# Retention and routed experts on one core: the routing counts kept as separate tiles, and scalings and weight splits moved between VectorE and GpSimd

## The chip, the cores and the metric

The kernel runs on one core of a Trainium2 chip. The metric is the device time of one execution in microseconds (us). TensorE, VectorE, ScalarE, GpSimd and SyncE are called PE, DVE, ACT, POOL and SP in the profile. SP issues nearly all loads, POOL issues the scatters by index.

## What is computed

Four sequences of 768 tokens with 8 heads of 64 features go through a retention layer: a state per head decays by a factor gamma at each token and takes up the product of key and value, and the output is the query times the state. The 3072 output rows of 512 features then go through a layer of 8 experts, each token to the one expert with the largest gate logit:

```python
for t in range(S):
    state = gamma * state + einsum('bhd,bhe->bhde', k[:, :, t], v[:, :, t])
    y[:, :, t] = scale * einsum('bhd,bhde->bhe', q[:, :, t], state)
...
logits = x @ w_gate
expert_idx = argmax(logits, axis=1)
...
for e in range(E):
    mask = expert_idx == e
    h = maximum(x[mask] @ w1[e], 0.0)
    out[mask] = gate_w[mask, None] * (h @ w2[e])
```

## The kernel before

**Two stages.** The first (roughly the first 103 us) does the retention, the gate logits and the sorting of the rows by expert into a DRAM tensor, `x_sorted`. The second (`moe_main`) takes one expert after the other and is a dense run of matmuls. Between them the first 320 rows of expert 0 are already multiplied as "early pieces" (`fill`, L801 and L820), so that TensorE has work while the last rows are routed.

**The first stage** works on 24 chunks of 128 tokens, six per sequence, in a hand-written order. The loop of L539 has twelve rounds, n = 0 to 11, with chunks a = 2n and b = 2n + 1 each. For a chunk g there are:

- `load(g)` (L222): one DMA of 1 MB with q, k and v, on SP's queue, which takes its instructions in order. Chunks 0 to 3, 15 to 18 and 21 to 23 use the four buffers `qkv_t`; the others use `qkv_w`, whose buffers are later those of the split weights.
- `scale(g)` (L237): `vs`, the values times a decay, one TENSOR_TENSOR with 128x512 outputs and both inputs in SBUF, on DVE or on POOL. There are three buffers for `vs`, so vs(g) waits until vs(g-3) was read for the last time.
- `scores(g)` (L250): matmuls into the PSUM tiles `sp` (L256), then the causal mask on DVE into `Sb` (L259, two instructions per chunk; one input is in PSUM).
- `update(g)` (L263): matmuls of the keys with vs(g) into the state `U` (L271), then a copy `ub` on ACT (L274). The next update writes the same `U`.
- `carry(n)` and `output(g)` (L290, L303): the output `Y`; `evict(g)` (L306): `Y` times a decay into `xT` on DVE (L311).
- `logits` (L351), `rows` (L322: transposes into the PSUM banks "s0" and "s1", which the scores use too) and `finish_logits` (L363, L367) of the round before.

**Routing** goes by six groups of chunks (`GROUPS`): the first 6 chunks are routed in round 3, the next 6 in round 6, then 4 in round 8, 2 in round 9, 4 in round 11 and the last 2 after the loop. In a group `choose` (L390 to L399, DVE) finds the expert of each token as a one-hot matrix `Eb`, `rank` (L406 to L410, PE) adds up in PSUM tile `pf` the row of each token inside its expert's region, `slots` and `weights` (DVE) take the row and the gate weight out, `label` (L438, L439, ACT) writes weight and token number into the row, and `advance` (L420) adds the group's counts to `run`: a TENSOR_REDUCE (L422) and a TENSOR_TENSOR (L423, `run` + `tot`). `run` starts as each expert's first row, divided by 128 (L601).

**Scatters.** `send_behind(tile, chunks)` (L328) lets POOL copy one column of `tile` (`gated`, L330), which makes it wait for that tile, and then issues one scatter of 128 rows per chunk (L746). `BEHIND`, `AMID` and `AFTER` (L46 to L48) say which chunks in which round. Round 9 is `soon`: after it all rows of the first 18 chunks are sent, and `fetch_early` (L454) reads the first 320 rows of expert 0 back, which `turn_early` (L458) transposes in round 11 into `xt0`.

**Weight splits.** `fetch(0, part)` (L123) loads a quarter of expert 0's weights into `raw`, which has two buffers; `split` (L133) makes `whi` on ACT (L138) and `wlo` on DVE or POOL (L139, both inputs in SBUF). In the first stage it does one of four pieces (128x512) at a time. `_PIECES` (L53) says how many pieces fall in which round; L620 does them at the end of it, on DVE in rounds 5, 7 and 10 and on POOL otherwise. The pieces go in the order part 0 to 3, piece 0 to 3. Parts 2 and 3 are fetched at chunks 6 and 8 (`fetches`, L534), which are reached at the ends of rounds 3 and 4; `LATER` (L52) has the loads of chunks 15 to 20 there too.

**Where the scalings stand before.** In rounds 3, 4, 6, 7 and 8 (`BEHIND`) POOL does vs(a+4) ahead of the round's scatters (L598), and DVE does vs(b+2) after the evictions (L604). In round 9 DVE does vs(b+2) there and POOL vs(a+4) after the scores. In the other rounds POOL does both after the scores (L617, L619).

Of the kernel before, what the change touches and what calls it, by code (L numbers as in the profile page):

```python
# [9 lines left out]
F32 = mybir.dt.float32  # L10
# [39 lines left out]
FIRST = AHEAD + 11  # L50
MID = (19, 20)
LATER = {6: (15, 16), 7: (17,), 8: (18,), 9: (19,), 10: (20,)}  # L52
_PIECES = {2: 3, 3: 2, 5: 4, 6: 1, 7: 2, 9: 2, 10: 2}  # L53
_ORDER = iter([(part, i) for part in range(4) for i in range(4)])
SPLITS = {n: tuple(next(_ORDER) for _ in range(c)) for n, c in _PIECES.items()}
BIG = 1 << 20
# [44 lines left out]
def retention_moe(ctx, tc, qkv, w1, w2, cst, gdec, out):  # L101
# [102 lines left out]
    with ExitStack() as actx:  # L204
# [168 lines left out]
        def gating(i):  # L373
            a, w = GROUPS[i]
            total = a + w in (FULL, NCH)
            last = a + w == NCH
            sm = lambda name, n=1, dt=F32: gsm.tile([P, w, n], dt, name=f"{name}{w}")
            bc = lambda t, n=E: t.broadcast_to([P, w, n])
            span = slice(a, a + w)
            Eb, key, gw = EA[:, span, :], KEY[:, span, :], GW[:, span, :]  # L380
            NB = w + total
            v = {}
            ex = exs[:, 0:w]

            def choose():

                lg, eq, pr = [state["spare"][:, n * w * E:(n + 1) * w * E].rearrange("p (i e) -> p i e", e=E)
                              for n in range(3)]
                mx, ed = v["mx"], v["ed"] = sm("mx"), sm("ed")
                nc.vector.tensor_reduce(out=mx, in_=lgs[i], axis=AX.X, op=ALU.max)  # L390
                nc.vector.tensor_reduce(out=lg, in_=lgs[i].unsqueeze(3), axis=AX.X, op=ALU.add)
                nc.vector.tensor_tensor(out=eq, in0=lg, in1=bc(mx), op=ALU.is_equal)
                nc.vector.tensor_tensor(
                    out=pr, in0=eq, op=ALU.mult,
                    in1=k_("desc").unsqueeze(1).broadcast_to([P, w, E]))
                nc.vector.tensor_reduce(out=ed, in_=pr, axis=AX.X, op=ALU.max)
                nc.vector.tensor_tensor(out=Eb, in0=pr, in1=bc(ed), op=ALU.is_equal)
                v["sh"] = sm("sh", E)
                nc.vector.tensor_tensor(out=v["sh"], in0=lg, in1=bc(mx), op=ALU.subtract)  # L399

            def soft():
                nc.scalar.activation(out=ex[:, :, 0:E], in_=v["sh"], func=AF.Exp)

            def rank():
                pf = v["pf"] = bank(2, "pf", (P, NB, E)) if i < 3 else ps_1.tile([P, NB, E], F32, name="pf", tag="U" if i == 4 else "misc")
                nc.tensor.matmul(out=pf[:, 0:w, :], lhsT=us, rhs=Eb, start=True, stop=False, skip_group_check=True)  # L406
                nc.tensor.matmul(out=pf, lhsT=ones, rhs=run.unsqueeze(1).broadcast_to([P, NB, E]),
                                 start=False, stop=False, skip_group_check=True)
                for n in range(NB - 1):
                    nc.tensor.matmul(out=pf[:, n + 1:, :], lhsT=ones,  # L410
                                     rhs=Eb[:, n:n + 1, :].broadcast_to([P, NB - 1 - n, E]),
                                     start=False, stop=(n == NB - 2), skip_group_check=True)

            def slots():
                rk = sm("rk", E)
                nc.vector.tensor_tensor(out=rk, in0=v["pf"][:, 0:w, :], in1=Eb, op=ALU.mult)
                with nc.allow_low_precision(reason="one nonzero term, an integer below 2**15"):
                    nc.vector.tensor_reduce(out=key, in_=rk, axis=AX.X, op=ALU.add)

            def advance():  # L420
                tot = gsm.tile([P, E], F32, name="tot")
                nc.vector.tensor_reduce(out=tot, in_=Eb.rearrange("p i e -> p e i"), axis=AX.X, op=ALU.add)  # L422
                nc.vector.tensor_tensor(out=run, in0=run, in1=tot, op=ALU.add)  # L423

            def counts():

                dst, classes = (cnt, slice(0, E)) if last else (full, slice(0, 1))
                nc.vector.tensor_tensor(out=dst, in0=v["pf"][:, w, classes], in1=k_("ebase")[:, classes],
                                        op=ALU.subtract)

            def weights():
                nc.vector.tensor_reduce(out=gw, in_=ex, axis=AX.X, op=ALU.add)
                nc.vector.reciprocal(out=gw, in_=gw)

            def label():
                b, c = divmod(a, CPB)
                x = xrows[b][:, c:c + w]
                nc.scalar.copy(out=x[:, :, :, P + 1], in_=gw.broadcast_to([P, w, 4]))  # L438
                nc.scalar.copy(out=x.bitcast(I32)[:, :, :, P],  # L439
                               in_=k_("tok4")[:, span].unsqueeze(2).broadcast_to([P, w, 4]))  # L440

            return dict(choose=choose, soft=soft, rank=rank, slots=slots, advance=advance, counts=counts,
                        weights=weights, label=label)

        early, first, start_at = [], {}, []

        def start_rows():

# [82 lines left out]
        scale(2)  # L531

        last = NCH // 2 - 1
        fetches = {6: 2, 8: 3}  # L534
        chosen = {(a + w) // 2: i for i, (a, w) in enumerate(GROUPS) if a + w < NCH}
        soon = FULL // 2
        stages = {}
# [1 line left out]
        for n in range(last + 1):  # L539
# [8 lines left out]
            if n > 0:  # L548
                if n == last:
                    turn_early()  # L550
                if n != soon:
                    logits(n - 1)
                if n == last:
                    for j, w, _ in first["pieces"]:
                        cut_high(nc, first["x"][0], first["xt"], j, w)
                if n in AMID:
                    send_behind(state["LT"][:, 0:1], AMID[n])
                rows(a - 2, "s0")
                rows(a - 1, "s1")
                finish_logits(n - 1)  # L560
            if s and n < last:
                s["choose"]()
            if n == soon:
# [30 lines left out]
            elif s:  # L594
                for name in ("weights", "label")[2 * (n == soon):] + ("advance",):
                    s[name]()
            if n in BEHIND:
                scale(a + 4)  # L598
                send_behind(xTs[n][:, 0, C:C + 1], BEHIND[n])
            if n == 1:  # L600
                nc.vector.tensor_scalar(out=run, in0=k_("ebase"), scalar1=1.0 / P, scalar2=None, op0=ALU.mult)  # L601
            if n < last:
                if n in BEHIND or n == soon:
                    scale(b + 2, nc.vector)  # L604
                if n > 0:
                    update(a + 2)
# [6 lines left out]
            if n == 0:  # L613
                nc.scalar.copy(out=wgs[:, :, 0:E], in_=k_("gates").rearrange("p (k e) -> p k e", k=NP))
            if n < last:
                if n not in BEHIND and n != soon:
                    scale(b + 2)  # L617
                if n < last - 1 and n not in BEHIND:
                    scale(a + 4)  # L619
            for i in SPLITS.get(n, ()):  # L620
                split(0, *i, nc.vector if n in (5, 7, 10) else nc.gpsimd, 1)
            for g in (a, b):
                if FIRST <= g < NCH - AHEAD - len(MID):
                    load(g + AHEAD + len(MID))
# [585 lines left out]
```

## Time and profile before

| what | us |
|---|---|
| median of 3 runs (lowest, highest) | 400.54 (398.85, 401.35) |
| the profiled execution, its own time | 400.35 |
| span of its profile, from the first to the last instruction | 398.5 |
| what lies around the span | 1.85 |
| busy: PE, DVE, POOL, ACT | 386.5, 248.7, 176.8, 141.7 |
| mean granted clock of PE, as a share of 2.4 GHz | 0.994 |

Times in the rows below are microseconds from the start of the span. A timeline row has start, duration, engine, line, operation, output tile "<-" input tiles, sizes and how often it is repeated without a break; in square brackets stands how long the engine was idle before it and what ended that. A repeated row's duration runs from the first start to the last end. Ends of matmuls are modelled, so the step from one PE row's start to the next is the safer measure.

### The profile page before, as it was taken

What the parts mean: (1) busy time and instruction counts of PE and PEld (TensorE: products, weight loads), DVE (VectorE), ACT (ScalarE), POOL (GpSimd) and SP (SyncE); (2) the same over time, 40 slices, a digit from 0 to 9 for tenths busy, and PEclk for the clock granted to TensorE, in tenths of its full rate; (3) what the DMA queues carried; (4) which work ended last, traced back from release to release, by engine and by line L of the source; (5) the groups of instructions that cost most, each with busy time, mean ns of one, the idle gap of its engine ahead of it and who ended that gap; (6) DMA issues with size and microseconds to landing.
All of it is one profiled execution on the core that took longest, in us unless ns stands there. A gap on an engine that the chain in (4) does not pass through costs nothing. (4 is left out here: it accounts for less than half of the span.)

```text
span 398.5 us, 8280 instructions
## 1 busy us (share of the span) xinstructions
PE 386.5 (97%) x3260; PEld 359.7 (90%) x3260; DVE 248.7 (62%) x479; ACT 141.7 (36%) x248; POOL 176.8 (44%) x168
## 2 busy tenths in 40 slices
PE   8999999879999999999999999999999999999995
PEld 4888878668899879999999999999999999999984
DVE  3467587986754578583877377467738656675411
ACT  2234344333511446532542345144324415523200
POOL 1647918581160417400483067118505822850743
PEclk9999999998999999999999999999999999999999
DMA  7999999963047939656443846365474737530111
GB/s 276 420 419 419 415 422 420 422 273 69 2 162 161 361 137 256 233 208 140 180 156 123 192 145 251 61 189 208 147 183 131 251 71 216 178 136 1 48 54 47
DMA packets 42332, 81.53 MB, mean 205 GB/s; under 512 B 4460, under 2 KB 18160, under 8 KB 39860
## 3 DMA queue, kind: packets, MB, share of 16 engines
q1 hardware_dynamic: 36768, 67.46, 50.3%
q0 software_dynamic: 5376, 13.49, 9.0%
q8 instruction: 26, 0.43, 0.4%
q14 instruction: 14, 0.11, 0.1%
q10 hardware_dynamic: 148, 0.04, 0.0%
HBM read 65.90 MB, written 15.68 MB: 205 GB/s over the span
## 5 line engine op out<-in xcount | busy, mean ns | idle before, releaser
L746 POOL DMA_INDIRECT out<-Z,sidx x90 | 102.8, 1143 | 138.8 <-DVE Z L927 113.5
L139 DVE TENSOR_TENSOR wlo<-raw,whi 128x1024 fp32r<-128x1024 f32 (+1 forms) x62 | 70.5, 1146 | 14.2 <-ACT whi L138 13.9
L138 ACT CAST whi<-raw 128x1024 fp32r<-128x1024 f32 (+1 forms) x72 | 67.4, 950 | 11.5 <-DMA raw<-w 9.3
L1071 PE MATMUL py<-hh,whi 128*128 128x452 f32 (+5 forms) x192 | 67.0, 349 | 0.0
L1071 PE MATMUL py<-hl,whi 128*128 128x452 f32 (+5 forms) x192 | 66.9, 349 | 0.0
L1071 PE MATMUL py<-hh,wlo 128*128 128x452 f32 (+5 forms) x192 | 66.8, 348 | 0.0
L1048 ACT ACTIVATE hh<-ph 128x452 fp32r<-128x452 f32 (+6 forms) x56 | 28.2, 506 | 81.1 <-PE ph L1043 81.1
L1049 DVE SCALAR_TENSOR_TENSOR hl<-ph,hh 128x452 fp32r<-128x452 f32 (+6 forms) x56 | 32.1, 574 | 29.3 <-ACT hh L1048 28.9
L1043 PE MATMUL ph<-xh,wlo 128*128 128x452 f32 (+6 forms) x224 | 50.2, 346 | 0.0
L1043 PE MATMUL ph<-xh,whi 128*128 128x452 f32 (+6 forms) x224 | 50.1, 346 | 0.0
L1043 PE MATMUL ph<-xl,whi 128*128 128x452 f32 (+6 forms) x224 | 50.0, 345 | 0.0
L1043 PEld LDWEIGHTS ph<-xh,whi 128*128 128x128 f32 x224 | 40.8, 188 | 0.8
L1043 PEld LDWEIGHTS ph<-xh,wlo 128*128 128x128 f32 x224 | 40.8, 188 | 0.7
L1043 PEld LDWEIGHTS ph<-xl,whi 128*128 128x128 f32 x224 | 40.7, 188 | 0.7
L1071 PEld LDWEIGHTS py<-hl,whi 128*128 128x128 f32 x192 | 36.1, 188 | 0.8
L1071 PEld LDWEIGHTS py<-hh,wlo 128*128 128x128 f32 x192 | 36.1, 188 | 0.7
L1071 PEld LDWEIGHTS py<-hh,whi 128*128 128x128 f32 x192 | 36.1, 188 | 0.7
L768 ACT CAST xh<-buf 128x512 fp32r<-128x512 f32 (+7 forms) x26 | 14.3, 555 | 57.2 <-DVE buf L761 57.2
L259 DVE TENSOR_TENSOR Sb<-sp,cs 128x512 f32<-128x512 f32 x48 | 29.9, 681 | 1.6 <-PE sp L256 1.6
L746 POOL DMA_INDIRECT x_sorted<-xrow,KEY x24 | 24.3, 1011 | 14.4 <-DVE lg L367 7.2
L922 DVE STREAM_TRANSPOSE Z<-py 128x416 f32<-128x416 f32 (+3 forms) x24 | 15.0, 626 | 24.3 <-PE py L1071 24.3
L775 DVE TENSOR_TENSOR xl<-buf,xh 128x512 fp32r<-128x512 f32 (+7 forms) x26 | 17.2, 660 | 15.8 <-ACT xh L768 15.8
(172 smaller groups left out, 543.2 us busy)
## 6 DMA issues: line engine op xcount, KB each, us to landing
raw<-w SPq DMA_DIRECT2D x32, 1024.0 KB, 5.2
qkv_w<-qkv SPq DMA_DIRECT2D x12, 1024.0 KB, 15.1
qkv_t<-qkv SPq DMA_DIRECT2D x7, 1024.0 KB, 14.6
qkv_t<-qkv SPq DMA_DIRECT2D x8, 512.0 KB, 7.2
buf<-x_sorted SPq DMA_DIRECT2D x12, 211.2 KB, 4.1
x_sorted<-cs SPq DMA_DIRECT2D x6, 260.0 KB, 6.5
buf<-x_sorted SPq DMA_DIRECT2D x8, 195.0 KB, 3.9
out<-Z,sidx POOLq DMA_INDIRECT x90
```

Source lines behind the costliest of these rows:

```text
L138: nc.scalar.copy(out=hi[:, h], in_=raw[:, h])
L139: engine.tensor_tensor(out=lo[:, h], in0=raw[:, h], in1=hi[:, h].bitcast(F32), op=ALU.subtract)
L259: nc.vector.tensor_tensor(out=Sb[:, r], in0=sps[r], in1=causal.unsqueeze(1).broadcast_to([P, NP, C]), op=ALU.mult)
L746: sc = tc.nc.gpsimd.indirect_dma_start(out=dst, out_offset=bass.IndirectOffsetOnAxis(ap=index, axis=0), in_=rows, in_offset=None, bounds_c ...
L768: nc.scalar.copy(out=xh[:, :, c0:c0 + w], in_=xt[:, :, t0:t0 + w])
L775: engine.tensor_tensor(out=xl[:, :, sl], in0=xt[:, :, t0:t0 + w], in1=xh[:, :, sl].bitcast(F32), op=ALU.subtract)
L922: nc.vector.transpose(out=Zs[e][:, 0:nb, k, :], in_=py[:, 0:32 * nb].rearrange("p (j c) -> p j c", c=32))
L1043: nc.tensor.matmul(out=ph[:, :cap], lhsT=wparts[e, f // 4][a][:, kd, fo:fo + P], rhs=x[:, kd, :cap], start=(n == 0), stop=(n == 3 * KD - 1))
L1048: nc.scalar.activation(out=hh[:, :cap], in_=ph[:, :cap], func=AF.Relu)
L1049: nc.vector.scalar_tensor_tensor(out=hl[:, :cap], in0=ph[:, :cap], scalar=0.0, in1=hh[:, :cap].bitcast(F32), op0=ALU.max, op1=ALU.subtract)
L1071: nc.tensor.matmul(out=py[:, :cap], lhsT=a[:, f % 4, k * P:(k + 1) * P], rhs=x[:, :cap], **se)
```

## The change

`advance` no longer adds to `run`. It makes a tile `tot{i}` of its own for each group, in BF16, and `rank` sums them on PE: one matmul more per earlier group. In round 8 POOL does vs(b+2) as well as vs(a+4) ahead of its scatters; in rounds 3, 4, 6 and 7 POOL's vs(a+4) goes behind the scatters, to the end of the round; in round 9 vs(b+2) goes from DVE to the end of the round on POOL. Splits: round 5 has three pieces, on POOL instead of DVE; round 7 has three, on DVE as before, but right after `finish_logits` instead of at the end; round 9 has four, on POOL; round 10 has none. Part 3 of the weights is fetched at chunk 11, the end of round 5, instead of chunk 8.

```diff
-_PIECES = {2: 3, 3: 2, 5: 4, 6: 1, 7: 2, 9: 2, 10: 2}
+_PIECES = {2: 3, 3: 2, 5: 3, 6: 1, 7: 3, 9: 4}
...
-                nc.tensor.matmul(out=pf, lhsT=ones, rhs=run.unsqueeze(1).broadcast_to([P, NB, E]),
-                                 start=False, stop=False, skip_group_check=True)
+                for part in [run] + tots:
+                    nc.tensor.matmul(out=pf, lhsT=ones, rhs=part.unsqueeze(1).broadcast_to([P, NB, E]),
+                                     start=False, stop=False, skip_group_check=True)
...
             def advance():
-                tot = gsm.tile([P, E], F32, name="tot")
-                nc.vector.tensor_reduce(out=tot, in_=Eb.rearrange("p i e -> p e i"), axis=AX.X, op=ALU.add)
-                nc.vector.tensor_tensor(out=run, in0=run, in1=tot, op=ALU.add)
+                tot = gsm.tile([P, E], BF16, name=f"tot{i}")
+                with nc.allow_low_precision(reason="an integer below 8"):
+                    nc.vector.tensor_reduce(out=tot, in_=Eb.rearrange("p i e -> p e i"), axis=AX.X, op=ALU.add)
+                tots.append(tot)
...
-        fetches = {6: 2, 8: 3}
+        fetches = {6: 2, 11: 3}
...
                 finish_logits(n - 1)
+            if n == 7:
+                for i in SPLITS[n]:
+                    split(0, *i, nc.vector, 1)
             if s and n < last:
                 s["choose"]()
...
+            if n == soon - 1:
+                scale(b + 2)
+                scale(a + 4)
             if n in BEHIND:
-                scale(a + 4)
                 send_behind(xTs[n][:, 0, C:C + 1], BEHIND[n])
...
             if n < last:
-                if n in BEHIND or n == soon:
+                if n in BEHIND and n != soon - 1:
                     scale(b + 2, nc.vector)
...
             if n < last:
-                if n not in BEHIND and n != soon:
+                if n not in BEHIND:
                     scale(b + 2)
-                if n < last - 1 and n not in BEHIND:
+                if n < last - 1 and n != soon - 1:
                     scale(a + 4)
-            for i in SPLITS.get(n, ()):
-                split(0, *i, nc.vector if n in (5, 7, 10) else nc.gpsimd, 1)
+            for i in SPLITS.get(n, ()) if n != 7 else ():
+                split(0, *i, nc.gpsimd, 1)
```

## Rows read from the trace of the kernel before

**Rows 1.** Busy time by stretch: start:end, length, engines (instructions), granted clock, DMA share, GB/s.
```profile
65.00:70.00 5.00, 5.00 (x111) 4.64 (x108) 3.37 (x4) 1.66 (x4) 4.38 (x7) 1.00 1.02 424
...
90.00:95.00 5.00, 4.79 (x54) 4.47 (x56) 2.17 (x5) 1.54 (x3) 0.38 (x1) 0.66 0.68 136
...
130.00:395.00 265.00, 263.37 (x1426) 253.77 (x1424) 162.80 (x247) 98.32 (x143) 113.51 (x98) 1.00 0.52 161
```

**Rows 2.** Timeline of PE in rounds 5 to 11, its waits among it.
```profile
50.01 0.64 PE L271 MATMUL U<-vs,qkv_w 128*64 128x64 f32 x16
...
55.71 0.44 PE L363 MATMUL lp<-cs,LT 128*128 128x128 f32 x2 [0.88 <-ACT LT L354]
...
64.14 0.69 PE L271 MATMUL U<-vs,qkv_t 128*64 128x64 f32 x16
...
66.41 0.64 PE L271 MATMUL U<-vs,qkv_t 128*64 128x64 f32 x16
...
74.56 0.17 PE L406 MATMUL pf<-EA,us 128*128 128x32 bf16 x1 [0.79 <-DVE EA L397]
74.59 0.18 PE L407 MATMUL pf<-run,ones 128*128 128x32 bf16 x1
...
78.33 1.25 PE L322 MATMUL tr<-cs,xT 128*128 128x128 f32 x8 [0.34 <-DVE Sb L259]
...
81.48 0.18 PE L406 MATMUL pf<-EA,us 128*128 128x16 bf16 x1 [0.46 <-DVE sh L399]
...
90.21 1.97 PE L322 MATMUL tr<-cs,xT 128*128 128x128 f32 x8 [2.53 <-DVE Sb L259]
...
92.53 1.11 PE L271 MATMUL U<-vs,qkv_t 128*64 128x64 f32 x16
...
103.08 0.85 PE L801 MATMUL ph<-xh,whi 128*128 128x320 f32 x4 [0.48 <-ACT xh L768]
```

**Rows 3.** Timeline of DVE in rounds 7 to 9.
```profile
67.83 1.71 DVE L240 TENSOR_TENSOR vs<-qkv_t,cs 128x512 f32<-128x512 f32 x1
...
71.86 1.28 DVE L139 TENSOR_TENSOR wlo<-raw,whi 128x512 fp32r<-128x512 f32 x2
...
84.95 0.16 DVE L422 TENSOR_REDUCE tot<-EA 128x8 f32<-128x16 bf16 x1
85.15 3.80 DVE L423 TENSOR_TENSOR run<-run,tot 128x8 bf16<-128x8 bf16 x1
```

**Rows 4.** Timeline of POOL: scalings, splits and scatters of rounds 4 to 9.
```profile
44.57 1.20 POOL L746 DMA_INDIRECT x_sorted<-xrow,KEY  x1 [0.30 <-DVE xT L311]
...
49.46 2.23 POOL L240 TENSOR_TENSOR vs<-qkv_w,cs 128x512 f32<-128x512 f32 x2
...
59.72 1.04 POOL L240 TENSOR_TENSOR vs<-qkv_t,cs 128x512 f32<-128x512 f32 x1 [8.03 <-DMA qkv_t<-qkv]
...
67.91 1.07 POOL L240 TENSOR_TENSOR vs<-qkv_t,cs 128x512 f32<-128x512 f32 x1
...
76.01 1.04 POOL L240 TENSOR_TENSOR vs<-qkv_w,cs 128x512 f32<-128x512 f32 x1 [3.95 <-DMA qkv_w<-qkv]
...
84.42 0.98 POOL L746 DMA_INDIRECT x_sorted<-xrow,KEY  x1 [0.30 <-issue]
85.41 1.07 POOL L240 TENSOR_TENSOR vs<-qkv_t,cs 128x512 f32<-128x512 f32 x1
86.41 2.50 POOL L139 TENSOR_TENSOR wlo<-raw,whi 128x512 fp32r<-128x512 f32 x2
```

**Rows 5.** Timeline of ACT in round 5.
```profile
51.02 1.66 ACT L138 CAST whi<-raw 128x512 fp32r<-128x512 f32 x3
...
54.76 0.62 ACT L138 CAST whi<-raw 128x512 fp32r<-128x512 f32 x1 [2.09 <-DVE Sb L259]
```

**Rows 6.** Timeline of SP: the first fetches of the early rows.
```profile
89.38 0.85 SPq L148 DMA_DIRECT2D xg<-x_sorted  x2
```

**Rows 7.** DMA issues of 75 to 90 us: output, queue, count, KB each, median us to landing.
```profile
xg<-x_sorted SPq DMA_DIRECT2D x2, 162.5 KB, 3.1
```

More of the change, by code (lines that the diff above doesn't have):

```diff
@@ L443, in gating @@
                         weights=weights, label=label)
-        early, first, start_at = [], {}, []
+        early, first, start_at, tots = [], {}, [], []
         def start_rows():
```

## The prediction

> **What bounds the kernel now.** I read first the busy times by stretch, then PE's timeline with its waits, then the timelines of DVE, POOL, ACT and SP around each wait. The reader is to see in the first view that the second stage is a closed run of matmuls: 263.4 of 265 us busy [rows 1]. Nothing there waits for the engines that the change touches, so whatever PE gains before about 103 us moves the whole rest forward, and the end with it; the routing chain of round 11 starts from PE's own outputs and moves along. In the first stage PE is nearly closed too, and the loads run at 424 GB/s with all DMA engines taken [rows 1]: so the order of loads matters, their sum doesn't change. What can be gained are PE's waits in rounds 6 to 11 [rows 2]: 0.88, 0.79, 0.34, 0.46, 2.53 and 0.48, together 5.5 us, and what the clock loses after the longest. After it the granted clock is 0.66 over 5 us [rows 1], that is, part of the stretch is at 1.2 GHz instead of 2.4.
>
> The long wait has its cause on DVE. L423, an addition of 8 columns per partition, lasts 3.80 us, from 85.15 to 88.95 [rows 3]. POOL meanwhile does a scaling and two splits without a pause, from 85.41 to 88.91 [rows 4]: DVE comes free when POOL's arithmetic ends. Both inputs of L423 are in SBUF. The same happens at 67.83: DVE's scaling, also with two SBUF inputs, takes 1.71 us, and POOL's scaling, from 67.91 to 68.98, lies inside it [rows 3, 4]; a split of the same size takes half of 1.28 on DVE [rows 3], so about 1.05 is lost. So a DVE instruction with two SBUF inputs stands still while POOL does arithmetic. Behind L423 stand a scaling and the masks, and PE's transposes wait for a PSUM bank that the first mask frees.
>
> **The change, part by part.** All against the profiled execution's own 400.35 us, which is 0.2 under the median of the three runs, 400.54.
>
> *L423 goes, and DVE's scaling of round 9 goes to POOL.* In round 9 DVE then has no instruction with two SBUF inputs: evictions and masks read PSUM, and L422 is a reduction of 0.16 us [rows 3] with one input. The masks start some 4.4 us earlier, before PE comes to the transposes: −2.5 for the wait. Late next would be U(21), whose scaling now stands behind POOL's scatters; the scatters end at 85.40 [rows 4], some 1.3 us earlier after the change (the sum of the terms of rounds 6 to 9 below), so that vs(21) and vs(22) are done near 85 and 86; PE needs the first at 92.53 less the gain, near 87.5 [rows 2]. Without the wait I expect no drop of the clock: the update took 1.11 instead of 0.69, 1.6 times as long, and by that ratio the 2.32 us from 90.21 to 92.53 were 1.44 of work at full clock [rows 2]; 0.42 and 0.88 are −1.3; if the clock falls all the same, that stays. L422 in BF16 has no row; its nearest is 0.16 in F32, and I take no difference (bounds ±0.2 per group, off the path).
>
> *More rank products.* 1+2+3+4+5 = 15 matmuls. One shows as a step of 0.03, from 74.56 to 74.59 [rows 2], its full duration is 0.18. So +0.5 (bounds 0.4 and 2.7); they are nearly always pipelined, which is why I take the step.
>
> *Round 5's splits go from DVE to POOL, the fourth goes to round 6.* ACT's fourth cast, 54.76, had waited 2.09 us for its buffer and held up `LT`, for which PE waited 0.88 [rows 5, 2]. With three casts ACT is free at 52.7: −0.9 (if the buffer wasn't the cause, 0). POOL takes 3 x 1.25 = 3.8 us more (half of the pair of 2.50) [rows 4], in a time of which it spends 8.03 us waiting for a load anyway, until 59.72 [rows 4].
>
> *vs(a+4) behind the scatters in rounds 3, 4, 6 and 7.* POOL does one scaling, 1.04 us, later in each. In round 4 this meets a due time: POOL's scalings after the scatters start at 49.46 [rows 4], so vs(12) ends at 50.50, and PE wants it for U(12) at 50.01 [rows 2]: +0.5 (bounds 0 and 1.04, the whole scaling). In rounds 3, 6 and 7 it is ready 1 us or more before its update.
>
> *Round 7's three splits right after `finish_logits`.* On ACT three casts, 1.66 us [rows 5], come ahead of the copy of U(15), which could start at 64.83, when U(15) ends [rows 2]. It then ends near 66.7, and U(16) at 66.41 must wait for it: +0.3 (bounds 0 and 1.7). On DVE the splits find POOL in arithmetic: the moved vs(16) and the split of round 6 come right after the scatters, so DVE loses about 1 us before its first split, and the eviction after them is some 1.5 us late. But DVE no longer loses 1.05 us at 67.83, where POOL now issues scatters, and the two splits ahead of the round's logits, 1.28 us at 71.86, are gone [rows 3]. The expert choice of round 8 so comes about 1 us earlier, and of PE's wait of 0.79 most goes: −0.7 (bounds −0.8 and +0.5).
>
> *Round 8: DVE's scaling goes to POOL.* Some 0.65 us less on DVE before the masks; PE's waits of 0.34 and 0.46 hang on these masks and the choice behind them [rows 2]: −0.5 (bounds 0 and −0.8). POOL had waited 3.95 us at this place for the load of chunk 20, until 76.01 [rows 4]. Now the loads of 18 to 20 are issued ahead of the weights' part 3, which SP had held back until round 5's splits were done. 1 MB at 424 GB/s is 2.5 us: chunk 20 lands by about 73.5. So POOL does both scalings before the eviction that starts its scatters.
>
> *Round 10 loses two splits on DVE*, 1.28 us ahead of the transposes of the early rows. PE's wait of 0.48 at 103.08 goes: −0.5. The rows must have landed: the fetch starts at 89.38 and takes 3.1 [rows 6, 7], so the rows land near 92.5 to 93.5, and 1.3 earlier after the change. The first early piece would come at 103.08 − 5.1 = 98 [rows 2], 6 us behind them where it was 10; transposes and casts stand between. If the rows came later than that allows, this term is lost first, and then PE waits us for us.
>
> A rule of the Trainium skill speaks to the scatters: SBUF — State Buffer, "Who interferes with whom", has it that a tensor_tensor with two SBUF inputs contends with GpSimd's reads of SBUF, and, as an inference, not with the writing of descriptors. Here a scatter that started while DVE did a scaling took 1.20 us, one without that 0.98 [rows 4]. By the page the splits beside scatters are free for POOL; by the rows three of them may put round 7's train 0.7 us back, which vs(18) just bears.
>
> The sum: −2.5 −1.3 +0.5 −0.9 +0.5 +0.3 −0.7 −0.5 −0.5 = −5.1, so 400.35 − 5.1 = 395.2 (rounded down).
>
> **The rivals.** (1) *The waits come back in another place.* DVE and POOL still meet in round 7; if DVE's splits are held through every piece of POOL's arithmetic and scatters, the waits of rounds 8 and 9 stay, +0.7 and +0.5, and the late eviction, which round 8's logits need, reaches PE with some 0.9 of its 1.5: −5.1 +2.1 = −3.0, 397.3. For it: the hold of 3.80 us was much longer than any single POOL instruction. Against it: two splits on DVE at 71.86 ran beside a scatter in 1.28, no longer than alone [rows 3].
>
> (2) *The hole isn't from POOL's arithmetic.* L423 started at 85.15, and POOL's scaling only at 85.41, after a scatter [rows 3, 4]. If something else holds DVE after the scatters, the next instruction is held, and wait and clock stay: −5.1 +2.5 +1.3 = −1.3, 399.0. Against it: the ends agree within 0.04 us. The same page of the Trainium skill says that whichever starts first gets the port and that the other blocks; by that L423 should have had it, and the rows here differ.
>
> (3) *More goes:* U(12) and the copy of U(15) find slack, and round 9's choice is early: −5.1 −0.5 −0.3 −0.3 = −6.2, 394.1.
>
> (4) *Slower: POOL's scatters wait for a load.* vs(19) and vs(20) now stand ahead of six scatters and, behind them, vs(21). If chunk 20 lands at T, vs(21) is ready at about T + 1.0 + 6 x 1.3 + 1.2 = T + 10. PE wants it at 87.5, so from T = 77.5 on each us costs one, and 1.3 more where the clock falls again. From T = 81.3 (3.8 late, and 1.3) nothing of the gain is left; at 83 the loss is 5.5 + 1.3 − 5.1 = 1.7, and at 85, 3.7 or 404.0. For it: this load was the one that POOL waited for, until 76.01 [rows 4]. Against it: it is now issued earlier and one load less is ahead of it.
>
> **How the numbers follow.** Forecast 0.57, rival (1) 0.18, (2) 0.10, (3) 0.09, (4) 0.06. The predicted time is 395.2. The range goes from 393.2, where rival (3) ends with a little to spare, to 399.0, where rival (2) lies; what is left out is (4), half of (2) and errors at the edges. A measurement can tell about 1%, 4 us, from no change. Under 396.5 are 0.53 of the forecast, rival (3) and a third of (1): 0.68. Slower by over 1%, above 404.5, is the far part of rival (4), and what I haven't thought of: 0.06. The rest, 0.26, is within 1%.
>
> **What would show it.** Right: no DVE instruction of round 9 above 1.4 us; no wait of PE before round 10's transposes and a granted clock of 1.00 throughout; PE's first early piece near 98; waits of some tenths at U(12) and U(16). Wrong: a new wait above 1 us in round 7 or 8 with a granted clock under 1, a wait of PE for vs(21), or DVE's transposes waiting for the early rows. If the first early piece comes 5 us earlier and the end doesn't, then the second stage was held by something other than PE.

## The result and the profile after

The kernel after takes 395.0 us (median of 4 runs, 394.64 to 395.4), the kernel before 400.58 (4 runs, 398.85 to 401.35): a ratio of 0.9867, with a 95% interval of 0.9833 to 0.9901. The forecast was 395.2. The profiled execution took 395.4 us, with a span of 393.5 (before 398.5) and a mean granted clock of 0.998 (before 0.994).

Three views carry the result. The first is what PE waited for over the whole run: line waited for, us in total, times, longest.

```profile
PE py L968 <- DVE hT L962: 1.1, 1, 1.1
PE warm L507 <- DVE ones L161: 1.1, 1, 1.1
PE pf L406 <- DVE sh L399: 0.3, 1, 0.3
PE Y L290 <- DVE xT L311: 0.2, 1, 0.2
```

Of the six waits of rounds 6 to 11 [rows 2] five are gone and one is cut to 0.33; `warm` is the start of the kernel, as before. The first line is in the second stage, where the forecast had none (the kernel before has one of 0.25 in that place, shown below). (L968 and L962 are L961 and L955 of before.)

The second view is PE's timeline of the kernel after. Its rows answer to [rows 2].

```profile
35.24 0.20 PE L406 MATMUL pf<-EA,us 128*128 128x48 bf16 x1
...
50.61 0.69 PE L271 MATMUL U<-vs,qkv_w 128*64 128x64 f32 x16
...
55.31 0.38 PE L363 MATMUL lp<-cs,LT 128*128 128x128 f32 x2
...
66.17 0.69 PE L271 MATMUL U<-vs,qkv_t 128*64 128x64 f32 x16
...
69.03 1.10 PE L290 MATMUL Y<-qkv_t,ub 64*64 64x128 f32 x32 [0.19 <-DVE xT L311]
...
73.78 0.19 PE L406 MATMUL pf<-EA,us 128*128 128x32 bf16 x1
...
80.06 0.18 PE L406 MATMUL pf<-EA,us 128*128 128x16 bf16 x1 [0.33 <-DVE sh L399]
...
80.12 0.22 PE L408 MATMUL pf<-tot,ones 128*128 128x24 bf16 x3
80.20 0.19 PE L411 MATMUL pf<-EA,ones 128*128 128x16 bf16 x2
...
86.27 1.09 PE L322 MATMUL tr<-cs,xT 128*128 128x128 f32 x8
...
87.51 0.69 PE L271 MATMUL U<-vs,qkv_t 128*64 128x64 f32 x16
...
97.06 0.85 PE L808 MATMUL ph<-xh,whi 128*128 128x320 f32 x4
...
135.45 0.72 PE L968 MATMUL py<-whi,hT 128*128 128x512 f32 x2 [1.11 <-DVE hT L962]
```

The transposes of round 10, 86.27, come without a wait and take 1.09 where they took 1.97; the update behind them takes 0.69 where it took 1.11 [rows 2]. The granted clock there is 1.00 (before 0.66 over 90 to 95 [rows 1]), in the busy times by stretch of the kernel after:

```profile
85.00:90.00 5.00, 5.00 (x103) 4.25 (x96) 1.58 (x4) 2.06 (x5) 5.00 (x6) 1.00 0.37 136
90.00:95.00 5.00, 5.00 (x96) 4.22 (x92) 4.04 (x7) 0.74 (x2) 2.19 (x2) 1.00 0.73 136
```

Follow one and the same instruction through both timelines, and the gain falls into legs. The first `pf`, of round 3, stands at 34.85 in the kernel before, in this row of PE's timeline:

```profile
34.85 0.20 PE L406 MATMUL pf<-EA,us 128*128 128x48 bf16 x1
```

| PE instruction | before | after | difference | on this leg | forecast |
|---|---|---|---|---|---|
| `pf` of round 3 | 34.85 | 35.24 | +0.39 | +0.39 | 0 |
| U(12) | 50.01 | 50.61 | +0.60 | +0.21 | +0.5 |
| `lp`, round 6 | 55.71 | 55.31 | −0.40 | −1.00 | −0.9 |
| U(16) | 66.41 | 66.17 | −0.24 | +0.16 | +0.3 |
| `pf` of round 8 | 74.56 | 73.78 | −0.78 | −0.54 | −0.7 |
| `pf` of round 9 | 81.48 | 80.06 | −1.42 | −0.64 | −0.5 |
| U(21) | 92.53 | 87.51 | −5.02 | −3.60 | −2.5 and part of −1.3 |
| first early piece | 103.08 | 97.06 | −6.02 | −1.00 | −0.5 and the rest of −1.3 |
| end of the span | 398.5 | 393.5 | −5.0 | +1.0 | 0 |

The 0.39 up to round 3 arose ahead of every row that the change moves; the two kernels of chip D below, one of before's order and one of after's, have this `pf` at 34.98 and 34.82, so it is start-up of this execution or scatter, and not a step of the change.

The third view is DVE and POOL around the places of the change. First DVE after; its rows answer to [rows 3], and two at the end belong to the late rows and to the second stage.

```profile
64.79 2.90 DVE L139 TENSOR_TENSOR wlo<-raw,whi 128x512 fp32r<-128x512 f32 x3 [0.74 <-ACT whi L138]
...
68.81 0.68 DVE L240 TENSOR_TENSOR vs<-qkv_t,cs 128x512 f32<-128x512 f32 x1
...
83.61 0.16 DVE L424 TENSOR_REDUCE tot<-EA 128x8 bf16<-128x16 bf16 x1
83.87 2.48 DVE L259 TENSOR_TENSOR Sb<-sp,cs 128x512 f32<-128x512 f32 x4
...
94.73 1.63 DVE L768 STREAM_TRANSPOSE xt<-xg 128x512 f32<-128x512 f32 x3 [0.72 <-DMA xg<-x_sorted]
...
131.86 2.93 DVE L782 TENSOR_TENSOR xl<-buf,xh 128x512 fp32r<-128x512 f32 x1 [1.68 <-ACT xh L775]
```

And POOL after, the same stretches, to be set against [rows 4].

```profile
64.63 1.29 POOL L139 TENSOR_TENSOR wlo<-raw,whi 128x512 fp32r<-128x512 f32 x1
...
66.68 1.30 POOL L753 DMA_INDIRECT x_sorted<-xrow,KEY  x1 [0.16 <-issue]
...
73.06 2.04 POOL L240 TENSOR_TENSOR vs<-qkv_w,cs 128x512 f32<-128x512 f32 x2
...
84.22 2.05 POOL L240 TENSOR_TENSOR vs<-qkv_t,cs 128x512 f32<-128x512 f32 x2
86.22 4.97 POOL L139 TENSOR_TENSOR wlo<-raw,whi 128x512 fp32r<-128x512 f32 x4
...
129.47 4.78 POOL L139 TENSOR_TENSOR wlo<-raw,whi 128x1024 fp32r<-128x1024 f32 x2 [1.72 <-ACT whi L138]
```

DVE's scaling of round 7, 1.71 in [rows 3], takes its own 0.68 now that POOL issues scatters there. In round 9 the four masks run at 83.87 right behind the reduction, in 2.48 us, while POOL does seven TENSOR_TENSORs without a pause from 84.22 on. Masks read PSUM and aren't touched. In the second stage one cut, L782 (the subtraction that makes `xl`, the low part of the rows, from `buf` and `xh`), has two SBUF inputs and lasts 2.93 instead of the 0.68 or so of such an instruction: it starts at 131.86, as POOL's second split begins, and ends at 134.79, 0.54 after it. Behind it stands `hT`, and for that PE waits 1.11.

The same place in the kernel before, in rows of DVE, POOL and PE (L775 is L782 of after):

```profile
137.61 0.89 DVE L775 TENSOR_TENSOR xl<-buf,xh 128x512 fp32r<-128x512 f32 x1 [1.68 <-ACT xh L768]
...
137.91 2.86 POOL L139 TENSOR_TENSOR wlo<-raw,whi 128x1024 fp32r<-128x1024 f32 x1
...
143.13 0.50 PE L961 MATMUL py<-whi,hT 128*128 128x512 f32 x1 [0.25 <-ACT hT L954]
```

Here too DVE's cuts and POOL's two splits meet. The first cut ends at 138.50, 0.55 after POOL's first split (135.55 to 137.95). POOL's second split follows without a pause, yet the cut got its turn, and the second split takes 2.86 where the first took 2.40. A second cut, at 139.50, stands until the second split is over (1.82 us), and PE waits 0.25 for the `hT` that comes after it.

### The profile page after: what moved, and what is told of

Its sections match the earlier page's. It is cut to its first block, busy times and chain, and to the rows that moved or that the text cites. A ratio compares the mean times of both kernels' runs of the same rounds, so it can differ in the third digit from the quotient of the medians.

```text
span 393.5 us, 8303 instructions
## 1 busy us (share of the span) xinstructions
PE 385.6 (98%) x3275; PEld 359.1 (91%) x3275; DVE 242.1 (62%) x467; ACT 141.3 (36%) x248; POOL 184.5 (47%) x175
## 4 chain that ended last, share of the span: by engine, by line
PE 94%; DVE 3%; issue 1%; ACT 1%; POOL 0%; POOLq 0%; DVEq 0%; ACTq 0%
PE ph L1050 31%; PE py L1078 27%; PE sp L256 5%; PE Y L303 5%; PE ph L808 4%; PE acc L827 4%; PE py L1076 3%; PE tr L322 3%; PE Y L290 3%; PE U L271 2%; PE L L351 2%; PE py L907 1%; PE py L968 1%; PE warm L507 1%; PE hn L951 1%
## 5 line engine op out<-in xcount | busy, mean ns | idle before, releaser
L139 DVE TENSOR_TENSOR wlo<-raw,whi 128x1024 fp32r<-128x1024 f32 (+1 forms) x57 | 68.4, 1205 | 14.3 <-ACT whi L138 13.9
L1050 PE MATMUL ph<-xh,wlo 128*128 128x452 f32 (+6 forms) x224 | 50.1, 345 | 0.0
L1050 PE MATMUL ph<-xh,whi 128*128 128x452 f32 (+6 forms) x224 | 50.1, 345 | 0.0
L1050 PE MATMUL ph<-xl,whi 128*128 128x452 f32 (+6 forms) x224 | 50.0, 345 | 0.0
L1050 PEld LDWEIGHTS ph<-xh,whi 128*128 128x128 f32 x224 | 40.8, 188 | 0.9
L1050 PEld LDWEIGHTS ph<-xh,wlo 128*128 128x128 f32 x224 | 40.8, 188 | 0.8
L1050 PEld LDWEIGHTS ph<-xl,whi 128*128 128x128 f32 x224 | 40.7, 188 | 0.7
L775 ACT CAST xh<-buf 128x512 fp32r<-128x512 f32 (+7 forms) x26 | 14.3, 555 | 58.1 <-DVE buf L768 58.1
L782 DVE TENSOR_TENSOR xl<-buf,xh 128x512 fp32r<-128x512 f32 (+7 forms) x26 | 18.1, 695 | 15.8 <-ACT xh L775 15.8
```

The lines of the kernel that those rows point to most:

```text
L139: engine.tensor_tensor(out=lo[:, h], in0=raw[:, h], in1=hi[:, h].bitcast(F32), op=ALU.subtract)
L782: engine.tensor_tensor(out=xl[:, :, sl], in0=xt[:, :, t0:t0 + w], in1=xh[:, :, sl].bitcast(F32), op=ALU.subtract)
L1050: nc.tensor.matmul(out=ph[:, :cap], lhsT=wparts[e, f // 4][a][:, kd, fo:fo + P], rhs=x[:, kd, :cap], start=(n == 0), stop=(n == 3 * KD - 1))
```

## The experiments

Theory P is the forecast's: a DVE instruction with two SBUF inputs that meets arithmetic of POOL stands still until POOL's unbroken run of it is over, and round 9's hole (DVE's sum of 3.80 us and PE's wait of 2.53 behind it) came from this alone. The rivals: DVE was held by something else, or by another rule (each expectation below names its own, as R, F or S), and what was won came from the other moves.

The runs fell on four chips. Call them B, C, D and E; whether the first measurement's chip is one of them isn't known. The kernel before takes 409.37 us on B (median of 31 runs), 407.06 on C (25), 400.43 on D (13) and 414.49 on E (7). On B, C and E the runs of the kernel before spread over 7 to 10 us (on D over 1.9), and the kernels run there show waits of PE that neither the first measurement nor D has.

### The kernel before once more (chip D)

> The kernel before, once more, for its trace on this chip. In the run that the prediction was made from, the sum L423 started 0.26 us ahead of GpSimd's scaling and was held 3.80 us. If the race has gone the other way here, as in the three traces of experiments where two-input instructions of round 9 started 0.8 to 0.9 us ahead: L423 takes 0.17 us, TensorE has no wait for the mask before round 10's transposes and its clock doesn't fall there; the change then has nothing to win in round 9. If the hold is there in full, the first explanation stands and something else eats the gain on this chip.

One run of 400.46 us. The hole is there again. DVE's row of round 9 in this run:

```profile
85.17 3.80 DVE L423 TENSOR_TENSOR run<-run,tot 128x8 bf16<-128x8 bf16 x1
```

3.80 us to the hundredth, as in [rows 3], and PE's wait is 2.53 again. So the hole isn't an accident of one execution.

### The sum put back into the kernel after, between the masks (chip D)

```diff
+                tot = v["tot"] = gsm.tile([P, E], F32, name="tot")
+                nc.vector.tensor_reduce(out=tot, ...)
+                if i != 3:
+                    add_total()
...
                 scores(a + 2)
+                if n == soon:
+                    s["add_total"]()
```

> The changed kernel with the running sum restored, and in round 9 issued between the masks of chunk 20 and those of chunk 21, which falls into GpSimd's unbroken arithmetic whatever the chip: the price of the hold where the masks stand behind it. Theory P: the sum is held until GpSimd pauses, 5 to 7 us; the masks of chunk 21 follow, and TensorE waits 4 to 6 us for them at the output of chunk 21, with its clock falling afterwards for another 1 to 1.5: 5 to 7.5 us above the changed kernel, ratio 1.011 to 1.018 to the kernel before where the changed one has 0.9987, or 0.999 to 1.005 where it has 0.987. Theory F (the port is given away after each instruction): under 1.3 us, not to be measured.

400.37 us (10 runs, 399.69 to 401.39), ratio 1.001 [0.9996, 1.0024]. All the moved scalings and splits of the change are in this kernel, and the gain is gone. DVE in its round 9, then POOL, then PE:

```profile
84.72 7.09 DVE L427 TENSOR_TENSOR run<-run,tot 128x8 bf16<-128x8 bf16 x1
...
83.85 2.05 POOL L240 TENSOR_TENSOR vs<-qkv_t,cs 128x512 f32<-128x512 f32 x2
85.85 4.93 POOL L139 TENSOR_TENSOR wlo<-raw,whi 128x512 fp32r<-128x512 f32 x4
90.75 1.03 POOL L240 TENSOR_TENSOR vs<-qkv_t,cs 128x512 f32<-128x512 f32 x1
...
92.47 0.44 PE L303 MATMUL Y<-Sb,vs 128*64 128x128 f32 x4 [3.75 <-DVE Sb L259]
```

An addition of 8 columns is held for 7.09 us. It ends at 91.81 and POOL's last scaling at 91.78. Seven POOL instructions follow each other, and DVE gets no turn between any two of them. PE then waits 3.75 us for the second pair of masks (expected: 4 to 6). Against the kernel after, by the two ratios, the hold costs 1.001 − 0.9867 = 1.4%, some 5.7 us, about the whole gain of the change. The kernel after wasn't run on D, so this sets ratios of two measurements against each other.

### The same sum behind all four masks (chip C)

The only difference to the kernel above is that the addition is issued after the four masks, so that it starts later in the same run of POOL.

```diff
-                if n == soon:
-                    s["add_total"]()
...
+            if n == soon:
+                s["add_total"]()
```

> The changed kernel with the running sum restored, but in round 9 the sum is issued behind the four masks, in the middle of GpSimd's two scalings and four splits (84.2 to 92.2 there), where nothing waits for it. This measures the hold by itself. Theory P with a hold through the whole unbroken run of GpSimd's arithmetic: the 8-column sum lasts from about 86.4 until that run pauses, 4 to 6 us. Theory F (the port goes to whoever comes next after each instruction): at most one GpSimd instruction, under 1.3 us. Rival R (a fixed cost of the sum): 3.8 us. TensorE sees nothing of it.

One run of 406.91 us. Rows of DVE and POOL:

```profile
97.12 5.00 DVE L427 TENSOR_TENSOR run<-run,tot 128x8 bf16<-128x8 bf16 x1
...
94.13 2.05 POOL L240 TENSOR_TENSOR vs<-qkv_t,cs 128x512 f32<-128x512 f32 x2
96.13 4.97 POOL L139 TENSOR_TENSOR wlo<-raw,whi 128x512 fp32r<-128x512 f32 x4
101.05 1.04 POOL L240 TENSOR_TENSOR vs<-qkv_t,cs 128x512 f32<-128x512 f32 x1
```

The end is 102.12 against POOL's 102.09. Three starts, three lengths (3.80, 5.00, 7.09), and each time the end of POOL's run: in round 9 P holds, and a fixed 3.8 us (R) and a turn after each POOL instruction (F) both fall there. As a rule for the whole kernel P is too strong: the cut at 137.61 in the kernel before (above) had to wait for one split only. The expectation that PE sees nothing failed: the eviction stands behind the sum, and PE waits 1.26 us for `xT`.

### The counts as tiles, and nothing else (chips B and E)

The kernel before with `advance` and `rank` changed as in the change, and no instruction moved.

```diff
+                    for part in [run] + tots:
...
-                nc.vector.tensor_tensor(out=run, in0=run, in1=tot, op=ALU.add)
+                tots.append(tot)
```

> The kernel before with only the counts as separate tiles summed by the rank products; all scalings and splits where they were. Theory P: the next VectorE instruction with two SBUF inputs, the scaling of round 9, takes the sum's place at about 85.15 and is held until GpSimd's arithmetic ends near 88.9; masks, TensorE's wait of 2.5 and the fall of the clock stay; 400.5 (399.5 to 401.5). Rival R: the hole goes with the sum, 396.5.

On B: 408.88 us, ratio 1.0041 [0.9989, 1.0094]. DVE's scaling took the place of the sum, at 92.35, and POOL's arithmetic began only at 93.17: nothing met, so the run tells nothing on the theory. It went again:

> The kernel before with the counts kept as tiles and nothing moved, once more, since the first time it ran where the next instruction of VectorE came 0.8 us ahead of GpSimd's arithmetic. Theory P (an instruction of VectorE with two SBUF inputs that meets GpSimd's unbroken arithmetic is held until that ends): where the kernel before runs at about 400 us, VectorE's scaling of round 9, L240, comes right behind the reduction, near 85.1 us, in the place of the sum, and is held to near 88.9 (3.5 to 3.9 us): PE's wait for the masks stays at 2.4 to 3.2 us and the time at 0.998 to 1.006 of the kernel before. Rival R (the sum itself, or its reading of the counts, was what took long): the scaling takes 0.7 to 1.1 us, PE's wait goes and the time is 0.985 to 0.992. If the scaling starts 0.5 us or more ahead of GpSimd's arithmetic, both expect no hold, and the run tells nothing between them.

On E: 415.09 us, ratio 1.012 [0.9986, 1.0253]; no time can be read from that. The profile is of the longest of the four runs, 419.93 us. But here the two did meet. DVE, POOL and PE in round 9:

```profile
92.32 4.16 DVE L240 TENSOR_TENSOR vs<-qkv_t,cs 128x512 f32<-128x512 f32 x1
...
92.42 1.06 POOL L240 TENSOR_TENSOR vs<-qkv_t,cs 128x512 f32<-128x512 f32 x1
93.42 2.50 POOL L139 TENSOR_TENSOR wlo<-raw,whi 128x512 fp32r<-128x512 f32 x2
...
97.14 0.55 PE L322 MATMUL tr<-cs,xT 128*128 128x128 f32 x3 [1.29 <-DVE Sb L259]
```

Without the sum, the scaling behind it is held in its place: 4.16 us, to 96.48, which is POOL's end at 95.92 and 0.56 more, most of the scaling's own 0.68. So the sum is nothing special, and the rival of this expectation is out: the next DVE instruction with two SBUF inputs is held as the sum was. PE's wait is back at 1.29 (P had said 2.4 to 3.2, for a chip where PE comes as early as in the first measurement). Where the two engines meet, tiles alone don't free the masks; DVE's scaling had to leave as well.

### The sum back, or POOL kept free, on a chip where they don't meet (chip B)

Two kernels. The first is the kernel after with `advance` and `rank` as before. The second is the kernel before with round 9's two splits on DVE:

```diff
-                split(0, *i, nc.vector if n in (5, 7, 10) else nc.gpsimd, 1)
+                split(0, *i, nc.vector if n in (5, 7, 9, 10) else nc.gpsimd, 1)
```

> The changed kernel with only the running sum restored: L423's addition is back on VectorE, the rank products use one count tile again; all moved scalings and splits stay. Theory P (port): a VectorE instruction with two SBUF inputs stands still while GpSimd does arithmetic. In the changed kernel the sum would start near 83.8 us, during the last scatter (83.22 to 84.20), and GpSimd then does two scalings and four splits without a pause until 92.2. If the sum is caught as in the kernel before, it lasts about 8 us, TensorE waits 5 to 6 us before round 10's transposes, the clock falls, time 402 to 404. Rival R (the hole belongs to the sum itself, 3.8 us whatever GpSimd does): wait 2.5, time 399. Rival F (whoever starts first has the port): the sum takes 0.2, time 395.

> The kernel before with one edit: the two splits of round 9 are done by VectorE instead of GpSimd, so that GpSimd has only one scaling (1.04 us) after the scatters. The sum L423 stays. Theory P: L423 is held until the one scaling ends, 1.2 to 1.4 us instead of 3.80; TensorE's wait before round 10's transposes falls from 2.53 to under 0.3, the clock stays at 1.00, time 396.3 to 397.3. Rival R: 3.8 us as before, 400.5.

407.64 us, ratio 0.9961 [0.991, 1.0011], and 406.75, ratio 0.9968 [0.992, 1.0016]: neither can be told from the kernel before. The rows of the first say why, DVE's sum and then POOL:

```profile
91.18 0.17 DVE L423 TENSOR_TENSOR run<-run,tot 128x8 bf16<-128x8 bf16 x1
...
91.09 0.98 POOL L751 DMA_INDIRECT x_sorted<-xrow,KEY  x1 [0.30 <-issue]
92.09 2.05 POOL L240 TENSOR_TENSOR vs<-qkv_t,cs 128x512 f32<-128x512 f32 x2
```

The sum starts 0.91 us ahead of POOL's arithmetic and is done in 0.17 (the second kernel has 91.16 and 0.17 likewise). As tests of the hole both missed. They show one thing: the sum ran its whole length beside a scatter and wasn't held, which speaks against rival (2) of the prediction.

### Round 7's splits back at the end of the round (chip B)

```diff
-            if n == 7:
-                for i in SPLITS[n]:
-                    split(0, *i, nc.vector, 1)
...
-            for i in SPLITS.get(n, ()) if n != 7 else ():
-                split(0, *i, nc.gpsimd, 1)
+            for i in SPLITS.get(n, ()):
+                split(0, *i, nc.vector if n == 7 else nc.gpsimd, 1)
```

> The changed kernel with round 7's three splits back at the end of the round, still on VectorE. Theory P: they meet GpSimd's scalings of 72.05 to 75.1 and stand ahead of round 8's logits, so that TensorE waits 1.6 to 2.8 us for the expert choice, against 0.4 saved at U(16) and carry: 396.4 to 398.5. Rival (splits beside scatters or at the end are the same to within the measurement): 395.0.

409.52 us, ratio 1.0066 [1.0012, 1.0119]. DVE's splits, POOL's scaling beside them, and PE in round 8:

```profile
76.14 3.07 DVE L139 TENSOR_TENSOR wlo<-raw,whi 128x512 fp32r<-128x512 f32 x3
...
76.40 1.06 POOL L240 TENSOR_TENSOR vs<-qkv_t,cs 128x512 f32<-128x512 f32 x1
...
80.64 0.18 PE L406 MATMUL pf<-EA,us 128*128 128x32 bf16 x1 [0.90 <-DVE EA L397]
```

Three splits take about 1.9 (three halves of the 1.28 of [rows 3]); 3.07 is 1.15 more, POOL's scaling of 1.06. The wait of round 8 is back, 0.90, less than the 1.6 to 2.8 I had expected. In the kernel with the sum back, on the same chip and with the splits in the early place, PE comes to this `pf` without a wait. So the early place is what takes the wait away; it stands at 0.79 in [rows 2]. What it is worth in time can't be said, since the kernel after wasn't run on B.

### The kernel after on another chip, and two tries to beat it (chips C and E)

> The changed kernel once more, as the measure for the runs beside it. If the chip is like that of the first measurement: ratio 0.985 to 0.989, 395. If it is like that of the first four experiments, where the kernel before takes 409 and TensorE's instructions come late near 86 to 89 us, so that GpSimd's arithmetic starts 0.8 us after VectorE's two-input instructions and holds nothing: the gain is what is left without the long hold, 1 to 2 us, ratio 0.995 to 0.998.

407.62 us, ratio 0.9987 [0.9945, 1.0029]: on C the kernel after wins nothing that can be measured. Its PE waits there for other things, as these lines of its waits show:

```profile
PE lp L363 <- ACT LT L354: 2.7, 3, 1.1
...
PE Y L303 <- issue: 1.0, 1, 1.0
```

"issue" is idle time that nothing in the profile explains. The kernel before kept no profile on C. Its relatives on B don't have the hole (above), so that there was less to win; whether that is the case on C too wasn't measured, and neither was why instructions come late on these chips.

The first try takes POOL's two splits of expert 1 away from the cut that they hold at 131.86: ACT's part stays, DVE does the subtraction in the late block. The load of expert 1's part 2 (`fetch(1, 2)`) moves to the late block with it, so it isn't a try of the subtraction alone. The second adds that round 6's POOL split goes ahead of its scatters.

```diff
-            split(1, 0, i, nc.gpsimd)
-        fetch(1, 2)
+            split(1, 0, i, None, 2, "h")
...
         prep(1, "turn")
+        for i in range(2):
+            split(1, 0, i, nc.vector, 2, "l")
+        fetch(1, 2)
```

> The changed kernel with the two splits of expert 1's first weights done by VectorE, after its first two transposes of late_block, instead of by GpSimd. In the changed kernel VectorE's cut of xl stands 2.93 us (131.86 to 134.79) beside them, and TensorE waits 1.11 us for hT. Theory P: without GpSimd's arithmetic the cut takes 0.7; the splits take 2.4 on VectorE, 1.3 to 1.7 of it in its idle time; TensorE's wait falls to 0 to 0.4, and the time by 0.6 to 1.1 us. Rival: VectorE's own 2.4 us delay the cut as much as the hold did: same time.

> As e6, and round 6's one split on GpSimd goes ahead of that round's scatters, so that in round 7 VectorE's splits meet only one scaling of GpSimd. Theory P: the three splits take 2.0 instead of 2.90 us, and the 0.2 us waits at U(16) and at round 8's carry shrink by 0.2 to 0.4 together; 0.8 to 1.5 us under the changed kernel in all.

> The kernel after with the first two low splits of expert 1 done by VectorE inside the late block instead of by GpSimd, once more, since the first time it ran where GpSimd's split ended before the cut of VectorE came. Theory P: where the kernel before runs at about 400 us, PE's wait of 1.11 us for hT goes to 0.4 or less, the cut of L782 takes 1.3 us or less instead of 2.93, and the time is 0.984 to 0.986 of the kernel before, 0.5 to 1.1 us under the kernel after. Rival S (VectorE has no slack there, so that the two splits of 0.65 us each put the cut as late as the hold did): the wait stays at 0.8 us or more and the time is 0.986 to 0.989.

On C 408.99 us, ratio 1.005 [1.0007, 1.0094], and 408.77, ratio 1.0073 [1.0034, 1.0111]; on E the first try again, 413.77, ratio 1.01 [0.9976, 1.0224]. All three missed in time. On C the three splits of round 7 take 1.90 in the second try, but they take 1.90 in the kernel after as well; and POOL's split ends at 142.39 in the kernel after and its cut starts only at 143.46, so that there was nothing to free in either place. On E the cut took 0.69 and PE had no wait for `hT`, but there is no run of the kernel after on E to set it against. Whether it wins the 1.1 us where the kernel after loses them stays open.

## Why the prediction was right

*The hole and the clock* (−2.5 and −1.3): right in place, cause and size. From `pf` of round 9 to the first early piece PE gained 4.60 us; the three terms there say 4.3. Both halves of the edit were needed: with a sum among POOL's arithmetic of round 9 the hole returns (chip D, 7.09 us), and without the sum the scaling is held in its place (chip E, 4.16 us). The direct test, the kernel before with less of POOL's arithmetic behind the scatters, ran only on a chip where the two don't meet. Rival (2) is out by the ends of three holds and by the sum that ran beside a scatter.

*Rank products* (+0.5): about right. Three of them step from 80.12 to 80.20, 0.03 each as said. Only 6 of the 15 come ahead of the first early piece, some 0.16. The other nine come among early pieces: from the `pf` of their round to the next early piece PE takes 0.41 and 0.24 us where before it took 0.31 and 0.12, so they cost 0.22 in the last leg, without a wait.

*Round 5's splits* (−0.9): −1.00 on the leg; `lp` has no wait. *U(12)* (+0.5): right, though its leg shows only +0.21. POOL's row of after, and PE's of the kernel of chip D with the sum between the masks:

```profile
49.48 3.06 POOL L240 TENSOR_TENSOR vs<-qkv_w,cs 128x512 f32<-128x512 f32 x3
...
50.30 0.69 PE L271 MATMUL U<-vs,qkv_w 128*64 128x64 f32 x16 [0.15 <-POOL vs L240]
```

The first of the three is vs(12). It ends near 50.5, as reckoned, and U(12) starts right behind it, at 50.61, which is 0.60 later than before. PE had come 0.39 late by itself, so that only 0.21 was left to wait; on chip D the profile names that wait. *U(16)* (+0.3): +0.16. ACT's three casts at 64.13 to 65.80 put the copy of U(15) to 66.07, and U(16) starts at 66.17; the copy was quicker than the 66.7 reckoned.

*Round 7* (−0.7): −0.54. DVE's splits lost 1 us to POOL's split as said (2.90 for three), the eviction came late, and PE shows it as a new wait of 0.19 for `xT`. The scatter beside them took 1.30 us against 0.98 (a like row of before has 1.20). The Trainium skill (SBUF — State Buffer, "Who interferes with whom") infers that a tensor_tensor doesn't disturb the writing of descriptors; this scatter differs, while another, at 44.53 of the kernel after, took only 1.03 beside a whole scaling of DVE. *Rounds 8 and 9* (−0.5): −0.64 on the leg, of which 0.34 is one wait gone, and 0.46 became 0.33 only.

*The early rows* (−0.5): the wait is gone, but the step under it failed. I had the rows land 1.3 us earlier, since the scatters end at 84.20 instead of 85.40. The first fetch starts at 89.37, as before [rows 6], and DVE waits 0.72 for it until 94.73; ACT's casts end at 97.00 and PE starts at 97.06. The cover that I took for 6 us is nearly used up. What SP waited for ahead of the fetch stands in its waits of the kernel after:

```profile
SPq L148 <- DMA x_sorted<-xrow,KEY: 5.4, 1, 5.4
```

These are the scatters' own transfers. Before, the wait was 4.3: the scatters were issued 1.2 us earlier and landed no earlier. The DMA engines are as good as full up to then in both kernels (from 75 to 80 and from 80 to 83 shares of 1.02 and 1.01 after, 1.01 and 0.96 before); that this held the transfers back wasn't tested.

*The second stage* (0): wrong by 1 us. The forecast said that nothing there waits for the engines that the change touches, and that a gain before 103 us moves the rest forward and the end with it. But in the kernel before DVE's cuts already met POOL's splits for expert 1, and PE waited 0.25. After the change they meet elsewhere: the cut ahead of `hT` comes as the second split begins and is held through it (2.93 us, PE waits 1.11). From the first `hn` to the first dense product of expert 1 (`ph`, L1043 before, L1050 after) PE takes 13.33 us (127.78 to 141.11) instead of 12.77 (133.53 to 146.30), so this place accounts for some 0.6 of the 1.0. The rank products are 0.2 more, and the last 0.2 lies spread over the 250 us behind and isn't explained. It is rival (1) in a place that I hadn't looked at, at 0.6 us of its 2.1.

So that the sum came so near is in part luck. Without the 0.3 for the nine late rank products the forecast has −5.4 up to the first early piece, and it was −6.0; behind it the forecast has those 0.3, and it was 1.0. Two errors of 0.6 and 0.7 cancel. Rival (4) didn't come: vs(19) and vs(20) run at 73.06 with no wait for chunk 20.

## What to carry to other kernels

Where a tiny VectorE instruction with two SBUF inputs shows microseconds, look for GpSimd arithmetic and compare the two ends: if they agree, the price isn't the instruction's. In round 9 it grew with the length of GpSimd's unbroken run; one cut in the second stage was let through after a single split. Take all such instructions out of the stretch, since the next in line is held in the place of the one removed; reductions and masks that read PSUM can stay. When the first stage gets shorter, look at the second for pairs of this kind whose meeting moves.

## What the runs showed of the hardware

In round 9 the hold lasts through GpSimd instructions of 512 columns that follow each other without a pause: 3.80, 4.16, 5.00 and 7.09 us for instructions that take 0.17 or 0.68 alone. Between two splits of 1024 columns in the second stage of the kernel before, which follow each other as closely, a VectorE instruction got its turn (0.89 us), and so it did in both traces of chip D (0.79 and 0.71 us): each time it ended 0.54 or 0.55 us after the first split, and the second took 2.86 or 2.87 us instead of 2.4. What makes the difference isn't known. A start in the profile ahead of GpSimd's doesn't protect: 0.26 us (the sum, [rows 3, 4]) and 0.10 us (the scaling on chip E) were not enough. Where it was 0.8 or 0.9 us, the instruction was done before GpSimd began. The Trainium skill (SBUF — State Buffer, "Who interferes with whom") says that whoever issues first gets the shared pair and that the other blocks; by the starts shown these runs differ, by the complete block they agree.

The same pair of kernels has the ratio 0.9867 [0.9833, 0.9901] in the first measurement and 0.9987 [0.9945, 1.0029] on chip C, where the kernel before takes 407.06 us. A gain that hangs on two engines meeting within 0.3 us may be one only where they meet; on C that wasn't seen in a trace of the kernel before.
